# Pair 0's k on two queues, its two heads gated apart, and SyncE's loads beside the weights tied to VectorE

## Chip, core and metric

The kernel runs on one core of a Trainium2 chip. The metric is device time in microseconds for one launch. The kernel before has a median of 290.4 us over 3 runs (288.86 to 292.19). The engines are called as in the profile: PE (TensorE matmuls), PEld (its weight loads), DVE (VectorE), ACT (ScalarE), POOL (GpSimd) and SP (SyncE). SP, ACT and POOL can each issue DMAs on a queue of their own.

## What is computed

Block-sparse attention over q, k, v of 4 x 8 x 768 x 64, and on its output a Fourier mixing layer with an MLP.

```python
# attention: 12 blocks of 64 keys
k_rep = k.reshape(B, H, 12, 64, D).mean(axis=3)
gate = einsum('bhsd,bhnd->bhsn', q, k_rep)            # causal by block
mask = top 3 blocks of each row by gate, and its own block, and causal
attn = softmax(where(mask, q @ k.T / 8, -1e9)) @ v
x = attn.transpose(0, 2, 1, 3).reshape(4, 768, 512)
# per batch element
u = x + real(fft(fft(x, axis=1), axis=2))
un = (u - mean(u)) / sqrt(var(u) + 1e-6)
out = u + maximum(un @ w_ch1, 0) @ w_ch2
```

## The kernel before

Work goes in 16 pairs of heads, four pairs to a batch element. A pair takes these steps (function `attention`):

- Loads of k, q and v of both heads (`load`, issued from L655), on SP but for the first ones of q.
- Casts to f16 (L1017 is the helper for VectorE and POOL, L1016 for ACT) and low halves, so that q and k are kept as a high and a low f16 part (`tensor_tensor` at L768 for q, L773 for k).
- The turn of k and q on PE (L785, L851) through PSUM, or for pairs from 7 on with DMA transposes on SP (L793, L842).
- Block sums of k, `k_sums`: pairs 0 to 2 take the f32 keys straight into PE (L809, `sums32 = p < 3`), later ones the two f16 parts (L814). `spread` (L831) copies the sums.
- The gate: `gates` (L871, 20 small matmuls for both heads in one PSUM bank), two additions on VectorE (L894, L898), ten MAX8 (`tops`, L905), a comparison with the third largest (L923), the turn of the resulting mask on PE (`m_turn`, L933), and `spell`, which writes it into extra rows of turned q (L943). The heads share one buffer for each step.
- Six groups of `scores` per head (L967), the causal mask, the exponential on ACT (L979), and `attend` (L997) with its normalization (L1006, L1009). The causal mask is a PE matmul with a triangle for pairs 0 to 4 (L962, `on_pe = p < 5`) and an affine select on POOL after the exponential for later ones (L985).

After every fourth pair follow `fourier` (stage 1 at L1072, stage 2 at L1106 to L1118), the normalization (L1162, L1165, L1189, L1193), a turn of the normalized rows `unT` (PE, L1213, or a DMA transpose at L1205) and the MLP (`up`, L1316, `down`, L1345). The last two batch elements use a seven-product scheme for `down` (L1289). The weights arrive as 16 transfers of 256 KB on POOL's queue (`weight`, L659).

The order of all this is not written by hand. Every step is an `Op` with a rank, costs per engine, what it reads and writes, and for transfers a duration; `Plan.schedule` places them one by one on engines and PSUM banks with a model of time, steered by tables of tuned ranks and choices (`RANKS`, `RELS`, `TAKES`). The result is a fixed order per engine, and instructions then wait for their operands only. So the planner's start times order the work, but nothing holds an instruction back until its planned time, except waits on data. Two details matter here:

- Where the planner sees PE idle in the first 75 us, it notes a count of fillers (`o.fill`), and as many matmuls of 512 columns on a zero tile run there (`filler`, L677). A first block of 12 stands ahead of all work.
- The planner models the transfers of SP and POOL as sharing the DMA engines: an SP transfer beside a POOL transfer lasts up to six times as long (`SHARE`).

The functions that the change touches, with the lines of the profile:

Of the kernel before, what the change touches and what calls it, by code (L numbers as in the profile page):

```python
# [16 lines left out]
NEG = -60000.0  # L17
AF = mybir.ActivationFunctionType
OP = mybir.AluOpType

S = 768
DM = 512
NB = 12
NST = 6
# [62 lines left out]
class Plan:  # L87
# [8 lines left out]
    LANDING = 0.8  # L96
    TURN = dict(alone=0.4, early=1.5, mixed=0.5)
# [60 lines left out]
    def schedule(self):  # L158
        ops = self.ops
        free = dict(PE=1.0, ACT=1.5, DVE=0.9, POOL=1.3, SP=0.75)  # L160
# [21 lines left out]
        port_free, holder = 0.0, None  # L182
# [8 lines left out]
        while left:  # L191
# [63 lines left out]
            if o.dma or o.turn:  # L255
# [7 lines left out]
                if o.turn and shared == 0.0:  # L263
                    o.done = max(free[e] + 1.4, dma_free[mine] + 3.0)
                o.base = dma_free[mine] = go + took
                landing[e].append(o)
                flying[other] = [d for d in flying[other] if d.base > go]
# [36 lines left out]
SPELL = 7  # L304
WBR, HAR = 17000, 19000
STEP = 13.4

# [16 lines left out]
for _c in CHUNKS:  # L324
# [214 lines left out]
def kernel(  # L539
# [9 lines left out]
    nc = tc.nc  # L549
# [133 lines left out]
    for i in range(2):  # L683
        small(0.5, "DVE", 0.2, lambda x, n, i=i: nc.vector.memset(gmp[i], 0.0), w=[("gmp", i)])
# [740 lines left out]
```

## Time and profile before

| | us |
|---|---|
| median of 3 runs | 290.4 (288.86 to 292.19) |
| profiled execution | 288.77 |
| its span, first to last instruction | 287.1 |
| PE busy | 281.5 (98%) |
| DVE busy | 231.7 (81%) |
| ACT busy | 177.5 (62%) |
| POOL busy | 165.6 (58%) |
| DMA read and written | 28.58 MB and 6.29 MB |

A row of groups reads: line, engine, operation, what is written and read, shape, count, then busy time, mean duration in ns, and the idle time before with what ended it. A row of waits reads: who waited for whom, then us in total, how often, the longest. A row of the chain reads: start, duration, work. A row of stages reads: window, its length, busy time and count for PE, PEld, DVE, ACT and POOL, the granted PE clock, the DMA share and GB/s. A row of issues reads: what is loaded, queue, count, size, median us from issue to landing. PE's busy time counts fillers as work.

### The profile page before, as it was taken

How to read it: one execution, taken by the hardware profiler on the slowest of the kernel's cores; microseconds unless marked ns; L12 is line 12 of the kernel's file. 1: busy time of each engine (PE TensorE's matmuls, PEld its weight loads, DVE VectorE, ACT ScalarE, POOL GpSimd, SP SyncE). 2: the span in 40 equal slices, each digit the busy share in tenths (PEclk: the TensorE clock that was granted, in tenths of full speed). 3: DMA queues.
4: the chain of work that ended last, by engine and by line, in shares of the span. 5: the costliest groups of instructions: out<-in, count | busy, mean ns of one | idle time of the engine just before them, and what ended most of it. 6: DMA issues, size and time to landing. Idle time of an engine off the chain costs nothing.

```text
span 287.1 us, 8223 instructions
## 1 busy us (share of the span) xinstructions
PE 281.5 (98%) x3034; PEld 199.6 (70%) x3034; DVE 231.7 (81%) x783; ACT 177.5 (62%) x403; POOL 165.6 (58%) x300
## 2 busy tenths in 40 slices
PE   8999999999999999999999999999999999999995
PEld 4788877885656676566656686566677787866884
DVE  5678899889436788988564989999998999847895
ACT  2759988994734663987925596888775534365000
POOL 6587867926974734788889453754127972031300
PEclk9999999999999999999999999999999999999999
DMA  8999999999799889987899984563100032330032
GB/s 208 264 230 237 237 255 187 196 200 164 125 207 194 199 163 211 208 133 169 142 179 257 189 190 77 86 144 87 21 1 2 1 82 85 59 109 0 21 128 75
DMA packets 124057, 41.05 MB, mean 143 GB/s; under 512 B 115705, under 2 KB 120985, under 8 KB 124017
## 3 DMA queue, kind: packets, MB, share of 16 engines
q1 hardware_dynamic: 119536, 35.67, 59.6%
q0 software_dynamic: 3552, 4.56, 9.2%
q8 instruction: 24, 0.39, 0.6%
q10 hardware_dynamic: 928, 0.30, 0.4%
q14 instruction: 17, 0.13, 0.2%
HBM read 28.58 MB, written 6.29 MB: 121 GB/s over the span
## 4 chain that ended last, share of the span: by engine, by line
PE 88%; DVE 5%; ACT 5%; issue 1%; DVEq 0%; ACTq 0%
PE bank L1316 28%; PE bank L1345 14%; PE bank L1289 13%; PE bank L967 11%; PE bank L997 6%; PE bank L677 3%; ACT turned L979 2%; PE bank L1072 2%; PE bank L809 1%; PE bank L851 1%; PE bank L933 1%; PE bank L814 1%; PE bank L962 1%; PE bank L871 1%; ACT u L1016 1%
## 5 line engine op out<-in xcount | busy, mean ns | idle before, releaser
L979 ACT ACTIVATE turned<-bank 128x512 f16<-128x512 f32 (+1 forms) x192 | 89.2, 574 | 13.4 <-PE bank L967 13.3
L1316 PE MATMUL bank<-unT,w 128*128 128x384 f16 x512 | 89.2, 326 | 0.6 <-DVE unT L1017 0.5
L1328 ACT ACTIVATE hT<-bank 128x384 f16<-128x384 f32 x98 | 47.0, 492 | 38.6 <-PE bank L1316 38.0
L1316 PEld LDWEIGHTS <-w 128*128 128x128 f16 x512 | 48.6, 98 | 31.3 <-issue 1.5
L967 PE MATMUL bank<-turned,keys 76*128 76x128 f16 (+7 forms) x384 | 50.5, 259 | 0.0
L1345 PE MATMUL bank<-w,hT 128*128 128x512 f16 x192 | 46.9, 378 | 0.0
L967 PEld LDWEIGHTS <-keys 76*128 76x128 f16 (+1 forms) x384 | 28.8, 97 | 11.7 <-issue 0.4
L985 POOL TENSOR_SCALAR_AFFINE_SELECT turned<-turned 128x256 f16<-128x256 f16 (+1 forms) x44 | 22.4, 520 | 11.2 <-ACT turned L979 7.4
L1297 DVE TENSOR_TENSOR u<-u,bank 128x256 f32<-128x256 f32 x72 | 25.9, 413 | 3.6 <-PE bank L1289 2.3
L1345 PEld LDWEIGHTS <-hT 128*128 128x128 f16 x192 | 17.2, 97 | 15.8
L997 PEld LDWEIGHTS <-turned 128*128 128x128 f16 x672 | 23.8, 97 | 3.3
L1240 POOL TENSOR_TENSOR turned<-hT 128x384 f16<-128x384 f16 x14 | 12.5, 911 | 22.9 <-ACT hT L1328 12.3
L1289 PEld LDWEIGHTS <-turned 128*128 128x128 f16 x240 | 23.5, 98 | 2.9
L997 PE MATMUL bank<-small,turned 128*128 128x65 f16 x672 | 25.2, 193 | 0.0
L773 POOL TENSOR_TENSOR loads<-loads 128x384 f16<-128x384 f32 x24 | 21.9, 914 | 2.1 <-PE bank L814 1.2
L1017 POOL CAST small<-loads 128x384 f16<-128x384 f32 x28 | 13.9, 504 | 14.9 <-DMA loads<-in_v_dram 7.7
L1330 DVE TENSOR_SCALAR hT<-bank 128x384 f16<-128x384 f32 x30 | 16.5, 553 | 6.2 <-PE bank L1316 5.0
L943 DVE TENSOR_SCALAR turned<-bank 12x384 f16<-12x384 f16 (+2 forms) x50 | 18.2, 364 | 3.1 <-PE bank L933 1.8
L768 POOL TENSOR_TENSOR turned<-loads,turned 128x320 f16<-128x320 f32 x25 | 19.6, 792 | 1.5 <-DVE pm L1042 1.0
L1240 POOL TENSOR_TENSOR turned<-hT,hT 128x384 f16<-128x384 f16 x12 | 10.9, 913 | 15.6 <-DVE turned L1240 6.0
L1009 DVE TENSOR_TENSOR x<-bank,small 128x384 f16<-128x384 f32 x32 | 17.7, 553 | 0.5
L1289 PE MATMUL bank<-loads,turned 128*128 128x256 f16 x144 | 17.2, 273 | 0.0
(144 smaller groups left out, 491.1 us busy)
## 6 DMA issues: line engine op xcount, KB each, us to landing
loads<-in_k_dram SPq DMA_DIRECT2D x28, 192.0 KB, 3.8
loads<-in_v_dram SPq DMA_DIRECT2D x28, 192.0 KB, 3.6
loads<-in_q_dram SPq DMA_DIRECT2D x26, 192.0 KB, 3.8
w<-in_moe_w_ch_dram POOLq DMA_DIRECT2D x16, 256.0 KB, 8.4
out_dram<-u SPq DMA_DIRECT2D x12, 256.0 KB, 3.0
out_dram<-u SPq DMA_DIRECT2D x24, 128.0 KB, 1.7
hT<-in_k_dram SPq DMA_DIRECT2D x4, 192.0 KB, 3.8
hT<-in_q_dram SPq DMA_DIRECT2D x4, 192.0 KB, 3.9
```

The source lines that it names most:

```text
L768: lambda x, n, hi=hi, lo=lo, e=e: eng[x].tensor_tensor(out=lo, in0=qn[a][:, e, 1:NST], in1=hi[:, 1:NST], op=OP.subtract),
L773: lambda x, n, kh=kh, kl=kl, e=e: eng[x].tensor_tensor(out=kl, in0=kn[a][:, :, e, :], in1=kh, op=OP.subtract),
L967: nc.tensor.matmul(bank32[sp.bank][:, co:co + a1 - a0], KI[e][g3][0:ROWS[e], jt, :], QG[e][g3][0:ROWS[e], a0:a1], start=not added, stop=no ...
L979: lambda x, n, sp=sp, pt=pt, at=at, wid=wid: nc.scalar.activation(out=pt[:, at:at + wid], in_=bank32[sp.bank][:, 0:wid], func=AF.Exp, scal ...
L985: lambda x, n, pt=pt, at=at, nd=nd: nc.gpsimd.affine_select(out=pt[:, at:at + 128 * nd].rearrange("p (a c) -> p a c", a=nd), in_=pt[:, at: ...
L997: nc.tensor.matmul(o[:, st, 0:65], pt[:, col:col + 128], V16[v4][:, e, jt, 0:65], start=(i == 0), stop=(i == 20))
L1240: lambda x, n_: eng[x].tensor_tensor(out=dst, in0=x0, in1=x1, op=op),
L1289: nc.tensor.matmul(bank32[mp.bank][:, 0:256], lhs[:, z, :], rhs[:, z, :], start=(z == 0), stop=(z == 7))
L1297: lambda x, n, mp=mp, sign=sign, part=part: nc.vector.tensor_tensor(out=part, in0=part, in1=bank32[mp.bank][:, 0:256], op=sign),
L1316: nc.tensor.matmul(bank32[hp_.bank][:, 0:384], w1[:, dt, 128 * it:128 * it + 128], unT[:, dt, 384 * hf:384 * hf + 384], start=(dt == 0), s ...
L1328: nc.scalar.activation(out=o, in_=i_, func=AF.Relu)
L1345: nc.tensor.matmul(bank32[cp.bank], hT[hf][:, it, 128 * j:128 * j + 128], w2[:, it, :], start=(it == 0), stop=(it == NIT - 1))
```

## The change

It has these parts; the planner's tables of ranks and choices are replaced with it, so that the order on every engine is another.

1. First loads: k of both heads leads, one on SP's queue and one on ACT's; q of head 0 moves from ACT's queue to SP's second place. The first block of fillers has 8 matmuls for 12. POOL's constants may be issued earlier.
2. The planner's model of the first transfers (issued before 8 us) changes (`EARLY`): they land one after another over all queues.
3. `SPLIT = 1`: for pair 0 the gate runs per head, with a PSUM bank, additions, MAX8, comparison and turn for each, and with the second head's mask in the other mask buffer.
4. `sums32 = p < 2` and `on_pe = p < 4`: pair 2's block sums come from f16 parts, and pair 4's causal mask moves to POOL. The cast of pair 0's q may also run on ACT.
5. `HELD`: an SP instruction whose planned start lies between 36 and 76 us gets a wait on the VectorE instruction that the plan ends last before that start.

```diff
+    EARLY = 8.0
+    HELD = (36.0, 76.0)
...
-                o.fill = (0 if st < 6.5 else int(gap / 0.215) if st > 16.0 else
+                o.fill = (0 if st < 5.0 else int(gap / 0.215) if st > 16.0 else
...
-                if o.turn and shared == 0.0:
+                if st < self.EARLY:
+                    o.done = early = max(early, free[e] + (2.4 if e == "POOL" else 2.1)) + work
+                    shared, took = 0.0, o.done - self.AFTER[mine] - go
+                elif o.turn and shared == 0.0:
...
+SPLIT = 1
...
-    P.op(0, {"PE": 4.9}, lambda x, n: filler(12), r=["warm"], w=["spare"])
+    P.op(0, {"PE": 3.4}, lambda x, n: filler(8), r=["warm"], w=["spare"])
...
     load(0, 1, "k", 0)
-    load(0, -2, "q", 0, "ACT")
-    load(0, 1.2, "k", 1)
+    load(0, -2, "k", 1, "ACT")
+    load(0, 1.2, "q", 0)
...
-        on_pe = p < 5
-        sums32 = p < 3
+        on_pe = p < 4
+        sums32 = p < 2
...
+        for es in ((0,), (1,)) if p < SPLIT else ((0, 1),):
+            e0, e1 = es[0], es[-1] + 1
+            gi = (g2 + e0) % 2
+            gp = P.psum("tr")
+
+            def gates(x, n, es=es, gp=gp):
+                for e in es:
...
+            def tops(x, n, es=es):
+                for st in range(5):
+                    for e in es:
+                        nc.vector.max(out=mx8[g2][:, st, e, :], in_=gsb[g2][:, st, 12 * e:12 * e + 12])
...
+            if o.eng == "SP" and P.HELD[0] < o.start < P.HELD[1]:
+                by = max((d for d in P.ops if d.i in made and d.eng == "DVE" and
+                          made[d.i] is not None and d.done < o.start), key=lambda d: d.done)
+                tc.add_manual_dep(made[o.i].ins, made[by.i].ins.name, mybir.DependencyInfo(
+                    mybir.DependencyClass.Sync, mybir.DependencyReason.DATA), reason="held")
```

Over the whole program this takes 12 f32 passes of L809, four matmuls of L962 and five fillers out of PE's order (46 to 41) and adds 12 f16 matmuls of L814 and five transposes of L933; POOL gets four affine selects more (44 to 48).

More of the change, by code (lines that the diff above doesn't have):

```diff
@@ L159, in schedule @@
         ops = self.ops
-        free = dict(PE=1.0, ACT=1.5, DVE=0.9, POOL=1.3, SP=0.75)
+        free = dict(PE=1.0, ACT=0.8, DVE=0.9, POOL=1.3, SP=0.75)
         ready = {e: [] for e in free}
@@ L181, in schedule @@
         flying = dict(POOL=[], SP=[])
-        port_free, holder = 0.0, None
+        port_free, holder, early = 0.0, None, 0.0
         order = []
@@ L683 @@
     for i in range(2):
-        small(0.5, "DVE", 0.2, lambda x, n, i=i: nc.vector.memset(gmp[i], 0.0), w=[("gmp", i)])
+        small(0.5, "DVE", 0.2, lambda x, n, i=i: nc.vector.memset(gmp[i], 0.0),
+              w=[("gmp", i, 0), ("gmp", i, 1)])
     for i in range(NV):
@@ L733 @@
             dr["IndR"].ap().rearrange("n (s c) -> n s c", c=128),
-            [("kind", e, i) for i in range(NG)], 0.2, r=["kz"] if e == 0 else [], rel=4.0)
-    const(0.8, "POOL", ltri, dr["SM"].ap()[:, 392:520], ["sm2"], 0.3, 4.7)
+            [("kind", e, i) for i in range(NG)], 0.1, r=["kz"] if e == 0 else [], rel=2.3)
+    const(0.8, "POOL", ltri, dr["SM"].ap()[:, 392:520], ["sm2"], 0.1, 3.0)
     load(0, 1.87, "v", 0)
@@ L763, in attention @@
                   r=[("kn", a, e)], w=[("k16", h2, e)], port=True, rel=release(p))
-            small(base + 1, {"DVE": 0.37, "POOL": 0.52} if fast else {"POOL": 0.52}, 0,
+            small(base + 1, {"DVE": 0.37, "POOL": 0.52, "ACT": 0.46} if p == 0 else {"DVE": 0.37, "POOL": 0.52} if fast else {"POOL": 0.52}, 0,
                   lambda x, n, hi=hi, e=e: _copy(x, hi, qn[a][:, e]),
@@ L857, in attention @@
                   r=[tq], w=[("qg", e, g3), ("qm", e, g3)], ps=[tq])
-        gp = P.psum("tr")
-        def gates(x, n):
-            for e in range(2):
-                for st in range(1, NST):
-                    q_ = QG[e][g3][:, 128 * st:128 * st + 128]
-                    if wide:
-                        at = 48 * (st - 1) + 24 * e
-                        nc.tensor.matmul(bank32[gp.bank][:, at:at + 24], q_, G[g2][:, e, :],
-                                         start=True, stop=True)
-                        continue
-                    at = 24 * (st - 1) + 12 * e
-                    for i in range(2):
-                        nc.tensor.matmul(bank32[gp.bank][:, at:at + 12], q_,
-                                         G[g2][:, e, 12 * i:12 * i + 12],
-                                         start=(i == 0), stop=(i == 1))
@@ L874, in attention @@
-        P.op(base + 20, {"PE": 0.27 if wide else 0.54}, gates,
-             r=[("gh", g2)] + [(t, e, g3) for t in ("qg", "qm") for e in range(2)],
-             w=[gp], ps=[gp], pre=[("gsb", g2)])
-        half = lambda t: t.rearrange("p a (e n) -> p a e n", e=2)
-        raw = lambda: half(bank32[gp.bank][:, 0:120].rearrange("p (a c) -> p a c", a=5))
-        part = lambda i: bank32[gp.bank][:, 0:240].rearrange(
-            "p (a e i n) -> p a e i n", a=5, e=2, i=2)[:, :, :, i, :]
-        third = lambda: mx8[g2][:, :, :, 2:3].to_broadcast([128, 5, 2, NB])
@@ L926, in attention @@
-        gt = P.psum("tr")
-        by = 2 if p >= SPELL else 1
-        nj = 6 // by if by == 2 else 5
-        def m_turn(x, n):
-            for j in range(nj):
-                nc.tensor.transpose(bank16[gt.bank][0:64 * by, 128 * j:128 * j + 128],
-                                    gmp[g2][:, by * j:by * j + by, :].rearrange("p a c -> p (a c)"),
-                                    id16)
-        P.op(base + 24, {"PE": 0.06 * nj}, m_turn, r=["sm", ("gmp", g2)], w=[gt], ps=[gt])
-        for e in range(2):
-            def spell(x, n, e=e):
-                rows = QG[e][g3][64 - AT[e]:64 - AT[e] + NB, 128:S].rearrange("p (a c) -> p a c", a=5)
-                turned = bank16[gt.bank][:, 0:128 * nj].rearrange("p (j c) -> p j c", j=nj)
-                for i in range(by):
-                    at = 64 * i + 32 * e
-                    nc.vector.tensor_scalar(out=rows[:, i::by, :],
-                                            in0=turned[at:at + NB, 0:nj - i, :],
-                                            scalar1=-NEG, scalar2=NEG, op0=OP.mult, op1=OP.add)
-            small(base + 25, "DVE", 0.69 if by == 2 else 0.47, spell,
-                  r=[gt, ("qg", e, g3)], w=[("qm", e, g3)], ps=[gt])
```

136 lines of the change are left out of this document (90 added, 46 removed), and 381 rows, old and new, of tables (ACT, DVE, POOL, RANKS).

## The prediction

> **What bounds the kernel now.** I read the page first (busy shares, chain), then the waits of PE, then the table of stages, then the chain in the first 18 us and the transfers of 40 to 70 us.
>
> ```profile
> PE 281.5 (98%) x3034; PEld 199.6 (70%) x3034; DVE 231.7 (81%) x783; ACT 177.5 (62%) x403; POOL 165.6 (58%) x300
> ...
> PE 88%; DVE 5%; ACT 5%; issue 1%; DVEq 0%; ACTq 0%
> ```
>
> PE (TensorE) is busy for 281.5 of 287.1 us, and the chain that ended last lies on it for 88%. What PE waited for, as a list of all its waits:
>
> ```profile
> PE bank L677 <- DVE bsb L666: 1.3, 1, 1.3
> PE bank L1316 <- DVE unT L1017: 0.5, 1, 0.5
> PE bank L1213 <- DVE keys L1017: 0.4, 1, 0.4
> PE bank L1072 <- ACT small L1016: 0.2, 1, 0.2
> ```
>
> These four are 2.4 us, and 1.3 of them is the start. So PE's time is a sum of instructions: what leaves PE's order shortens the run, and a wait in PE's order lengthens it one for one. Part of this "work" is padding, though. The fillers (L677) are matmuls on zeros that the planner puts where it expects PE to be idle:
>
> ```profile
> L677 PE MATMUL bank<-bsb 128*128 128x512 f16 x46 | 13.7, 426 | 1.3 <-DVE bsb L666 1.3
> ```
>
> By stage (busy us of PE, PEld, DVE, ACT, POOL):
>
> ```profile
> 0.00:17.00 17.00, 15.73 (x152) 10.68 (x153) 11.16 (x66) 6.89 (x10) 10.63 (x26) 1.00 1.03 230
> 17.00:40.00 23.00, 22.96 (x407) 18.48 (x405) 19.59 (x74) 21.45 (x50) 17.84 (x30) 1.00 1.05 241
> 40.00:60.00 20.00, 19.82 (x266) 15.81 (x265) 18.45 (x64) 18.23 (x43) 16.90 (x27) 1.00 1.11 204
> 60.00:76.00 16.00, 15.18 (x170) 9.99 (x168) 12.39 (x45) 10.03 (x23) 9.04 (x17) 1.00 0.88 146
> ```
>
> From 17 to 40 us ACT's exponentials fill 21.45 of 23 us, so PE has little lead there. PE idles 0.18 us in 40 to 60 and 0.82 in 60 to 76.
>
> **The change, part by part.** The changed program has 41 fillers for 46: 8 ahead of the first real work for 12, and 33 later ones for 34. Of the later ones 15 stand ahead of pair 0's first scores for 17 before, and 18 behind them for 17.
>
> *The start.* Pair 0's key sums (L809) need both heads' k. Before, both k sit behind each other on SP's queue and q of head 0 heads ACT's; now k of head 1 heads ACT's queue.
>
> ```profile
> 1.27 4.57 PE bank L677 x12
> 5.84 1.30 PE bank L809 x12
> ...
> 12.75 1.94 PE bank L677 x9
> 14.69 0.40 PE bank L933 x5
> 15.09 0.60 PE bank L871 x20
> 15.69 1.34 PE bank L809 x12
> ```
> ```profile
> 0.82 0.48 ACTq L655 DMA_DIRECT2D loads<-in_q_dram  x1
> 0.82 1.03 SPq L655 DMA_DIRECT2D loads<-in_k_dram  x2
> ```
> ```profile
> loads<-in_q_dram ACTq DMA_DIRECT2D x1, 192.0 KB, 3.7
> loads<-in_k_dram SPq DMA_DIRECT2D x1, 192.0 KB, 3.3
> ```
> ```profile
> loads<-in_k_dram SPq DMA_DIRECT2D x1, 192.0 KB, 4.2
> ```
>
> The first rows give the issues, the others the time to landing: the heads of the two queues land at 0.8 + 3.3 = 4.1 and 0.8 + 3.7 = 4.5 us. The second k on SP, issued half-way through its 1.03 us, at 1.3, lands at 1.3 + 4.2 = 5.5. So both k are there at 4.5 instead of 5.5. Fillers start 0.42 us apart at first (rows below), so eight of them end at 1.27 + 8 x 0.42 = 4.65, when k is in. Twelve ended near 5.7, where the sums' first row stands.
>
> ```profile
> 4.24 0.15 PEld L677 LDWEIGHTS <-bsb 128*128 128x128 f16 x1 [0.28 <-issue]
> 4.66 0.15 PEld L677 LDWEIGHTS <-bsb 128*128 128x128 f16 x1 [0.28 <-issue]
> 5.03 0.32 PEld L677 LDWEIGHTS <-bsb 128*128 128x128 f16 x2 [0.22 <-issue]
> ```
>
> The start is 5.68 - 4.65 = 1.0 us earlier. But PE runs at half rate until about 5.03 us (0.42 us a filler against 1.94/9 = 0.216 later), and what now runs between 4.65 and 5.03 pays that: the sums lose half of 0.38, 0.2 us. Net 0.8 us gained. Counted as four fillers at 0.42 it would have been 1.7.
> The Trainium skill (TensorE: Matmul & The Clock Gate, "What's actually happening") says why: the warm-up is a budget of some 3.4 us of activity and not a number of matmuls, with a window that does not start with the kernel. This trace agrees, with 5.03 - 1.27 = 3.8 us, although the granted clock in the table of stages reads 1.00.
>
> *Heads gated apart (pair 0).* The gate matmuls stay 20 (10 and 10); the two heads' MAX8 stay 10; three VectorE instructions become six halves; the turn of the mask is done per head, so 5 more transposes of PE: at most 0.40 us, L933's row above. The VectorE halves run where PE had 9 fillers (the row at 12.75 us) and has 7 now, so these cover them; without that cover each would delay the mask's turn by its own length. One filler less in all: 0.2 us gained.
>
> *Pair 2's key sums in f16* (from `sums32 = p < 2`): 12 passes in f32 go, 1.34 us by the last L809 row, and 12 matmuls of two columns come, 0.28 us by the row below. 1.06 us gained. In exchange k's low halves are made by one more POOL and one more VectorE instruction.
>
> *Pair 4's causal mask* (from `on_pe = p < 4`): four PE matmuls go, two of 512 and two of 256 columns. L1345 streams 512 columns in 2.60/12 = 0.216 us (rows below), 256 take half: 0.65 us gained. POOL gets four affine selects.
>
> ```profile
> 79.69 0.28 PE bank L814 x12
> ...
> 83.30 2.60 PE bank L1345 x12
> ```
> ```profile
> L985 POOL TENSOR_SCALAR_AFFINE_SELECT turned<-turned 128x256 f16<-128x256 f16 (+1 forms) x44 | 22.4, 520 | 11.2 <-ACT turned L979 7.4 <-DVE small L824 0.9 <-DVE x L1193 0.9
> L773 POOL TENSOR_TENSOR loads<-loads 128x384 f16<-128x384 f32 x24 | 21.9, 914 | 2.1 <-PE bank L814 1.2 <-DVE fs L1029 0.9
> ```
>
> POOL's addition is 4 x 0.52 = 2.1 us for pair 4 and 0.9 for pair 2, at 17 to 60 us, where it has 23 + 20 - 17.84 - 16.90 = 8.3 us free. Bounds: 0 if it lies in those, 2.1 if all four selects delay pair 4's attend matmuls. With POOL as full as that PE idled only 0.18 us from 40 to 60; I take 0.2, nearest to that row.
>
> *The held transfers.* Seventeen issues of SP between the planner's 36 and 76 us get a wait on VectorE: the six loads of pair 7 and the six of pair 8, pair 7's four DMA transposes, and one transpose of the normalized rows. The first waits for pair 6's gate mask (L924 of the changed kernel). Everything later on SP queues behind it; pair 7's casts on POOL, and pair 7's key sums in PE's order, wait for it. SP before:
>
> ```profile
> 39.44 0.38 SPq L655 DMA_DIRECT2D loads<-in_k_dram  x1
> ...
> 45.21 10.81 SPq L655 DMA_DIRECT2D loads<-in_q_dram  x2
> 56.13 8.90 SPq L655 DMA_DIRECT2D loads<-in_k_dram  x2
> ```
> ```profile
> w<-in_moe_w_ch_dram POOLq DMA_DIRECT2D x14, 256.0 KB, 8.7
> loads<-in_q_dram SPq DMA_DIRECT2D x4, 192.0 KB, 14.5
> loads<-in_k_dram SPq DMA_DIRECT2D x3, 192.0 KB, 6.8
> ```
>
> Pair 7's loads went out at 39 to 45 us, among fourteen weight loads, and SP's landings took 6.8 to 14.5 us (medians of k and q). The planner had placed them at 61 us, which nothing enforced; now its places of 57 to 76 us for the seventeen are enforced by the waits. So pair 7's loads go out some 15 us later than they did, behind most of the weights' issues. PE idles 0.82 us in 60 to 76; the hold can give that back at most, and nothing at least if those waits (on VectorE's copies, second and third row of PE's waits) have nothing to do with transfers. I take half, 0.4. Its loss is a rival below.
>
> **The sum.** -0.8 (start) - 0.2 (one filler) - 1.06 - 0.65 + 0.40 (turns) + 0.2 (POOL) - 0.4 (hold) = -2.5 us. The profiled execution has 288.77 us, span 287.1; it becomes 286.3. The runs shown have a median of 290.4 (288.86 to 292.19), 1.6 over the profiled one; the forecast for the median is 290.4 - 2.5 = 287.9.
>
> **Rivals.**
> *The held loads land late (slower).*
>
> ```profile
> 65.89 7.31 PE bank L1316 x44
> ```
>
> Pair 7's key sums now stand behind 13 groups of `up` (four L1316 matmuls, 4 x 7.31/44 = 0.66 us), six score groups (up to 512 columns, 0.22 us) and two attends (21 matmuls of 65 columns each, at L1345's rate 0.58 us) counted from the first `up`: 8.6 + 1.2 + 1.2 = 11.0 us. The first `up` was at 65.9 and is some 2 us earlier now, so the sums are due at 75. POOL's low halves (0.91 us each, L773's row) and the casts ahead of them take some 2.8 us, an estimate; the loads must be in by 72. Issued at 58 to 62 they land at 65 to 69 with k's 6.8 us, which leaves 3 us, and at 73 to 77 with q's 14.5, which makes PE 1 to 5 us late: it takes its order as it stands. It decides once the loads are over 5.4 us late (2.5 gained, and 2.9 for 1%). With 14.5 us and a last issue at 65, if VectorE is late too, they are 7.5 late: 287.9 + 7.5 = 295.4. For it: SP's slow rows. Against: at 58 few weights fly.
> *The clock stays low.* If k or q come late, PE is idle just as its rate is to rise, and a second low stretch follows: 3.8 us at half rate, 1.9 us lost, 289.8. For it: the padding ahead of the key sums is cut to eight. Against: the head of ACT's queue landed at 4.5.
> By the same section of the Trainium skill (TensorE: Matmul & The Clock Gate) an idle window puts the clock back; a second stretch of its 3.4 us would cost 1.7 us, an estimate, and no run here shows one.
> *The early start is given back.* From 17 to 40 us ACT has 1.55 us free. If it sets the pace to 40 us, what is gained ahead of that (0.8 + 0.2 + 1.06) only makes PE wait: -0.4 remains, 290.0. For it: the changed order has 8 fillers where pair 2 is, which had 4. Against: those are in the count already, and ACT too starts earlier.
> *The hold also takes the runs' spread.* If PE's 1.0 us of idle time from 40 to 76 goes whole, POOL costs nothing, and the median comes down to the profiled execution: 288.77 - 2.3 - 1.0 = 285.5. For it: three runs differ by 3.3 us, and SP's landings among weights by as much. Against: no row ties the two together.
>
> **How the numbers follow.** Forecast 0.50, with its own range 286.2 to 289.2; loads late 0.10; clock low 0.10; given back 0.12; spread taken 0.18. About 1% (2.9 us) is what a measurement of this kernel can tell from no change: 287.5 and 293.3 are the bounds. Faster: 0.28 of the forecast and 0.18, together 0.46. Slower: 0.10. Within 1%: 0.44. The range leaves out the late loads and a tail below: 285.3 to 290.9.
>
> **What would show it.** Right: the first key sums at 4.6 to 4.8 us and the first scores near 14 us instead of 15.69 + 1.34 = 17.0, since pair 2's key sums and pair 1's gates no longer stand ahead of them; twelve L809 passes fewer; SP's first issue for pair 7 near 58 us, with landings under 8 us; PE idle under 1 us in 40 to 76. Wrong: a wait of PE on DMA or POOL near 75 us (late loads), fillers or sums 0.4 us apart after 5.5 us (clock), PE waiting for ACT between 17 and 40 us (given back).

## The result, and the profile after

The changed kernel has a median of 292.25 us (289.6 to 297.33, 20 executions) and the kernel before, measured beside it, 290.41 us (288.86 to 293.35, 20 executions). The ratio of the two is 1.005, with an interval of 1.0027 to 1.0074. It is slower by half a per cent, less than the 1% that separates two kernels here, and 2.5 us of forecast gain are missing. Executions over 1.5% above the fastest of their kernel are left out of the ratios (4 of 20 of the changed kernel, 1 of 20 of the kernel before), and where a profile below is of such an execution (e2, e11 and f3) only its start is read. The profiled execution after took 290.25 us, span 288.5, against 288.77 and 287.1 before.

Busy time and the chain that ended last, from the page after:

```profile
PE 280.8 (97%) x3030; PEld 198.5 (69%) x3030; DVE 229.8 (80%) x784; ACT 176.9 (61%) x402; POOL 173.2 (60%) x309
...
PE 75%; DVE 8%; DMA 7%; ACT 5%; POOL 2%; issue 2%; SPq 0%; DVEq 0%; ACTq 0%; POOLq 0%
```

PE lost only 0.7 us of busy time, and its share of the chain fell from 88% to 75%: DMA, DVE and POOL now stand on the path. What PE waited for, after:

```profile
PE bank L881 <- DMA turned<-turned: 1.5, 3, 1.2
PE bank L685 <- DVE bsb L674: 1.3, 1, 1.3
PE bank L1121 <- ACT tr L1031: 0.5, 1, 0.5
PE bank L1331 <- DVE x L1024: 0.4, 1, 0.4
PE bank L860 <- ACT turned L994: 0.3, 1, 0.3
PE bank L1228 <- ACT turned L994: 0.2, 1, 0.2
PE bank L1331 <- DVE u L1153: 0.2, 1, 0.2
```

The four waits of before (2.4 us) have become seven (4.4 us). The largest is new: L881, the gate of pairs that are turned by DMA transposes. The stages after (columns as before):

```profile
17.00:40.00 23.00, 22.59 (x410) 18.02 (x409) 19.93 (x80) 21.14 (x49) 19.63 (x31) 1.00 1.00 232
40.00:60.00 20.00, 19.38 (x300) 15.57 (x297) 18.39 (x75) 18.04 (x42) 15.65 (x30) 1.00 1.06 185
60.00:76.00 16.00, 15.79 (x180) 10.95 (x177) 11.72 (x33) 14.54 (x33) 12.84 (x20) 1.00 0.96 190
76.00:140.00 64.00, 62.47 (x621) 39.52 (x620) 44.36 (x159) 39.49 (x94) 40.52 (x83) 1.00 0.94 184
```
```profile
76.00:140.00 64.00, 63.98 (x676) 41.66 (x675) 47.54 (x160) 42.53 (x104) 43.88 (x88) 1.00 0.95 184
```

The last row is of the kernel before. Length less busy time is PE's idle time: 0.04 became 0.41 us in 17 to 40, 0.18 became 0.62 in 40 to 60, 0.82 became 0.21 in 60 to 76, and 0.02 became 1.53 in 76 to 140.

A busy PE can still be slow, so idle time is not all. To see both, each PE instruction is counted at the usual distance to its successor in the kernel before (the median of its kind), and the rest of the time is called lost. That count is an arithmetic on the whole trace, and an estimate. It gives some 274.5 us of work before and 272 after: the work fell by 2.5 us. The lost time rose by 4.0 us: 0.5 from 5 to 18 us, 1.2 from 18 to 70, 1.95 from 70 to 140, 0.3 after that.

The start, in the chain of the first 18 us, after:

```profile
1.27 3.60 PE bank L685 x8
4.87 1.57 PE bank L818 x12
...
11.51 1.51 PE bank L685 x7
...
14.61 0.22 PE bank L982 x2
```

Eight fillers, the sums right behind them, first scores near 14.5 us as forecast. SP's queue after:

```profile
59.28 0.38 SPq L663 DMA_DIRECT2D loads<-in_v_dram  x1
...
67.95 0.51 SPq L663 DMA_DIRECT2D loads<-in_v_dram  x1
68.76 2.25 SPq L851 DMA_TRANSPOSE turned<-turned  x1
```
```profile
SPq L663 <- DVE small L1180: 21.0, 1, 21.0
```
```profile
loads<-in_q_dram SPq DMA_DIRECT2D x4, 192.0 KB, 5.1
loads<-in_k_dram SPq DMA_DIRECT2D x3, 192.0 KB, 5.4
```

The hold did what it says: SP stood for 21.0 us behind one wait on VectorE, pair 7's loads went out from 59 us, and they landed in 5.1 to 5.4 us (medians from 40 to 72 us) and not in 6.8 to 14.5.

### The profile page after: what moved, and what is told of

The parts are those of the page before. It is cut to its first block, busy times and chain, and to the rows that moved or that the text cites. A ratio compares the mean times of both kernels' runs of the same rounds, so it can differ in the third digit from the quotient of the medians.

```text
span 288.5 us, 8239 instructions
## 1 busy us (share of the span) xinstructions
PE 280.8 (97%) x3030; PEld 198.5 (69%) x3030; DVE 229.8 (80%) x784; ACT 176.9 (61%) x402; POOL 173.2 (60%) x309
## 4 chain that ended last, share of the span: by engine, by line
PE 75%; DVE 8%; DMA 7%; ACT 5%; POOL 2%; issue 2%; SPq 0%; DVEq 0%; ACTq 0%; POOLq 0%
PE bank L1331 21%; PE bank L1360 13%; PE bank L1304 13%; PE bank L982 10%; PE bank L1012 6%; DMA turned<-turned 3%; PE bank L685 3%; ACT turned L994 2%; DMA hT<-in_k_dram 2%; DMA loads<-in_v_dram 2%; PE bank L860 1%; PE bank L948 1%; DVE x L1024 1%; PE bank L818 1%; PE bank L823 1%
## 5 line engine op out<-in xcount | busy, mean ns | idle before, releaser
L994 ACT ACTIVATE turned<-bank 128x512 f16<-128x512 f32 (+1 forms) x192 | 90.4, 579 | 20.8 <-PE bank L982 20.2
L1331 PE MATMUL bank<-unT,w 128*128 128x384 f16 x512 | 90.9, 326 | 0.6 <-DVE x L1024 0.4
L1343 ACT ACTIVATE hT<-bank 128x384 f16<-128x384 f32 x95 | 46.4, 501 | 39.6 <-PE bank L1331 34.6
L1331 PEld LDWEIGHTS <-w 128*128 128x128 f16 x512 | 48.0, 97 | 30.2 <-issue 1.3
L982 PE MATMUL bank<-turned,keys 128*128 128x128 f16 (+7 forms) x384 | 51.3, 258 | 0.2
L1000 POOL TENSOR_SCALAR_AFFINE_SELECT turned<-turned 128x512 f16<-128x512 f16 (+1 forms) x48 | 24.7, 524 | 17.1 <-ACT turned L994 7.7
L1255 POOL TENSOR_TENSOR turned<-hT 128x384 f16<-128x384 f16 x14 | 12.6, 912 | 22.7 <-ACT hT L1343 18.4
L1345 DVE TENSOR_SCALAR hT<-bank 128x384 f16<-128x384 f32 x33 | 18.3, 554 | 9.5 <-PE bank L1331 8.1
L1032 POOL CAST turned<-loads 128x384 f16<-128x384 f32 x25 | 12.6, 508 | 12.4 <-DVE fs L1069 8.7
L1032 POOL CAST small<-loads 128x384 f16<-128x384 f32 x24 | 12.1, 508 | 13.0 <-DMA loads<-in_v_dram 4.3
L1255 POOL TENSOR_TENSOR turned<-hT,hT 128x384 f16<-128x384 f16 x13 | 11.8, 914 | 11.8 <-DVE turned L1255 5.5
```

The lines of the kernel that those rows point to most:

```text
L982: nc.tensor.matmul(bank32[sp.bank][:, co:co + a1 - a0], KI[e][g3][0:ROWS[e], jt, :], QG[e][g3][0:ROWS[e], a0:a1], start=not added, stop=no ...
L994: lambda x, n, sp=sp, pt=pt, at=at, wid=wid: nc.scalar.activation(out=pt[:, at:at + wid], in_=bank32[sp.bank][:, 0:wid], func=AF.Exp, scal ...
L1000: lambda x, n, pt=pt, at=at, nd=nd: nc.gpsimd.affine_select(out=pt[:, at:at + 128 * nd].rearrange("p (a c) -> p a c", a=nd), in_=pt[:, at: ...
L1032: return eng[x].tensor_copy(out=dst, in_=src)
L1255: lambda x, n_: eng[x].tensor_tensor(out=dst, in0=x0, in1=x1, op=op),
L1331: nc.tensor.matmul(bank32[hp_.bank][:, 0:384], w1[:, dt, 128 * it:128 * it + 128], unT[:, dt, 384 * hf:384 * hf + 384], start=(dt == 0), s ...
```

## The experiments

Three theories stood against each other. *Hold*: the wait on SP costs more than it brings. *Start*: with eight fillers and k on both queues, PE's rate rises late in many executions. *Order*: the new order, and the work given to POOL, return what PE saves as waits on other engines. Ratios are to the kernel before, with a 95% interval.

### How well one comparison repeats

e0 is the changed kernel, unchanged, a second time.

> The changed kernel once more, beside the three that follow. All theories: 1.003 to 1.008 of the kernel before; PE waits for DMA transposes at the gate matmuls (L881), 1 to 2 us in all, and for ACT and VectorE between 30 and 66 us, some 2 us in all.

Measured: 291.27 us, ratio 1.0032 (1.0004 to 1.0061); PE's waits at L881 are 0.9 us in its profile. Three kernels were measured twice, on different chips. The changed one gave 1.0050 and 1.0032. The one without the hold (e1, e11) gave 0.9977 and 1.0005. The one of e5 and f6 gave 0.9974 and 1.0053, with intervals that do not meet. So a kernel's ratio moves by 0.2 to 0.8% from one measurement to the next, which the interval of one measurement does not cover. Below, a cause is called shown only where several kernels agree or where the profile has the place.

### The hold

e1 and e11: the changed kernel with

```diff
-    HELD = (36.0, 76.0)
+    HELD = (0.0, 0.0)
```

> The changed kernel without the waits of SP on VectorE (HELD = 0 to 0); the order on every engine is the same. Theory 'order' (the new order leaves the DMA transposes and ACT's exponentials too little time ahead of PE): PE's waits stay within 0.7 us of the changed kernel's, and the time within 0.3%. Theory 'hold' (held loads hand their lateness on to pair 7's transposes and all that follow): the waits at L881 near 81, 97 and 115 us go, and the time falls by 1.5 to 2 us, under the kernel before. If the hold does what it is written for, pair 7's loads go out from about 40 us instead of 59, land after 10 us and more, and the time rises by up to 1 us.

Measured: 0.9977 (0.9951 to 1.0003), 0.55% (1.6 us) under e0, measured beside it.

> The changed kernel without the hold once more: 0.995 to 1.000 of the kernel before. Theory 'hold': PE waits for DMA transposes at the gates of pairs 7 to 9 for under 1 us in all between 70 and 140 us. Theory 'order': over 1.5 us in this execution too.

Measured: 1.0005 (0.9978 to 1.0031). e6 does the reverse and gives the kernel before the same wait:

```diff
+    HELD = (36.0, 76.0)
...
+            if o.eng == "SP" and P.HELD[0] < o.start < P.HELD[1]:
+                by = max((d for d in P.ops if d.i in made and d.eng == "DVE" and
+                          made[d.i] is not None and d.done < o.start), key=lambda d: d.done)
+                tc.add_manual_dep(made[o.i].ins, made[by.i].ins.name, ...)
```

> The kernel before with the hold alone (same rule, same range of the planner's time); the order on every engine is the same. Theory 'hold' (held loads hand their lateness on to the DMA transposes behind them): slower by 0.3 to 0.7%, PE waits for DMA transposes or POOL between 70 and 140 us, over 1.5 us idle there for 0.8 before. Theory 'fit' (only the changed order has no time left for it): within 0.3%.

Measured: 1.0043 (1.0014 to 1.0071). The stages of 60 to 140 us of e6, then of e1:

```profile
60.00:76.00 16.00, 15.18 (x174) 10.30 (x172) 12.93 (x46) 10.44 (x23) 8.18 (x16) 1.00 0.96 184
76.00:140.00 64.00, 62.36 (x656) 40.14 (x655) 46.53 (x158) 40.28 (x97) 42.58 (x86) 1.00 0.96 184
```
```profile
60.00:76.00 16.00, 15.79 (x195) 11.13 (x193) 11.85 (x33) 14.84 (x35) 12.26 (x23) 1.00 0.73 128
76.00:140.00 64.00, 63.81 (x648) 40.58 (x644) 46.30 (x163) 41.05 (x98) 42.62 (x85) 1.00 0.90 184
```

In the order of before, the hold leaves the 0.82 us of 60 to 76 as they were and puts 1.64 us of idle time into 76 to 140. In the new order without it, 60 to 76 has 0.21 us all the same, and 76 to 140 has 0.19 instead of 1.53. So the new order took the idle time of 60 to 76, the hold none of it. f3 holds the loads alone, f4 (with `o.turn` for `not o.turn`) the DMA transposes alone:

```diff
-            if o.eng == "SP" and P.HELD[0] < o.start < P.HELD[1]:
+            if o.eng == "SP" and not o.turn and P.HELD[0] < o.start < P.HELD[1]:
```

> The changed kernel with the wait on VectorE left on the twelve loads of pairs 7 and 8 and taken from the DMA transposes. If the loads held back (and what queues behind them) are what costs: ratio as the changed kernel, 1.003 to 1.005, TensorE idle in 70 to 140 us near 2.5 us. If the wait of the transposes themselves costs: as without the hold, 0.998 to 1.0005, idle there near 0.7 to 1.5 us.

> The changed kernel with the wait left on the DMA transposes alone (pair 7's four and one of the normalized rows) and taken from the loads. If the held loads cost: 0.998 to 1.0005 and idle time in 70 to 140 us near 0.7 to 1.5 us. If the held transposes cost: 1.003 to 1.005 and idle time near 2.5 us.

Measured: f3 1.0035 (1.0005 to 1.0065), f4 1.0016 (0.9991 to 1.0042). The idle time of 76 to 140 alone does not prove the price, since e1 and f4 reach that stage more than 1 us later than the changed kernel (their start, next section). Two waits of PE that all kernels of the new order share make a measure without the start: the first at L1121, for ACT's copy in the first Fourier layer, and the one at L1331, for VectorE, near 179 us. From the second to the last matmul all eight need 106.0 us (in e8 the lines are L1126 and L1336).

| | loads held | wait at L1121 ends, us | wait at L1331 ends, us | between |
|---|---|---|---|---|
| after | yes | 56.44 | 179.19 | 122.75 |
| e0 | yes | 56.05 | 178.50 | 122.45 |
| f4 | no (transposes held) | 57.65 | 179.50 | 121.85 |
| e1 | no | 57.48 | 178.75 | 121.27 |
| e5 | no | 56.63 | 177.95 | 121.32 |
| e8 | no | 56.51 | 177.94 | 121.43 |
| f6 | no | 59.11 | 180.67 | 121.56 |
| e4 | no | 57.25 | 180.65 | 123.40 |

The stretch is some 1.1 us longer where the loads are held (mean 122.6) than in five of the six kernels where they are not (mean 121.5). The sixth, e4, has no hold and is the longest, with these waits for transposes:

```profile
PE bank L881 <- DMA turned<-turned: 1.8, 3, 0.8
```

So PE can wait there without a hold too. Over all: the changed kernel with the loads held (after, e0, f3) has a mean ratio of 1.0039, the same order without (e1, e11, e4, e5, f4, f6, of which e4, e5 and f6 have more fillers) 1.0005. By this the hold costs 0.34% or 1.0 us there, and 0.43% or 1.2 us in e6.

How a hold that ends at 76 us makes PE wait at 96 to 118 us shows in e6. One transpose in SP's queue, of before and of e6, and the waits of PE that e6 has and the kernel before has not:

```profile
92.23 1.29 SPq L842 DMA_TRANSPOSE turned<-turned  x1
```
```profile
95.17 1.29 SPq L843 DMA_TRANSPOSE turned<-turned  x1
```
```profile
PE bank L867 <- DMA turned<-turned: 0.8, 1, 0.8
...
PE bank L1317 <- DMA unT<-x: 0.5, 1, 0.5
...
PE bank L968 <- DMA keys<-loads: 0.4, 1, 0.4
```

The same transpose goes out 2.9 us later, and PE's wait of 0.8 us ends when it has landed. Of these 2.9 us, 1.0 are not the hold's: in this execution PE's rate rose late, and every matmul from 17 to 90 us stands 1.0 us later than before. The three new waits on transposes make 1.7 us. In the changed kernel the queue does not explain the price: from 79 to 110 us SP issues every transpose within 0.2 us of e1's time. The longest wait, 1.2 us at 115 us, is for a transpose that SP issued at the same time after and in e1:

```profile
109.86 1.45 SPq L851 DMA_TRANSPOSE turned<-turned  x1
```
```profile
109.83 1.21 SPq L851 DMA_TRANSPOSE turned<-turned  x1
```

By the trace it landed 5.4 us later after and 3.3 us later in e1, but 5.4 us later in e4 as well. Why it took longer stays open.

### The start

e4 takes e1 and puts the old first block back (`filler(12)` for `filler(8)`). e5 and f6 take e1 and add two fillers to each of the paddings that are planned between 5 and 9 us:

```diff
-            filler(o.fill)
+            filler(o.fill + 2 if o.fill and 5.0 < o.start < 9.0 else o.fill)
```

> The changed kernel without the hold, and with 12 fillers in the first block as before the change. Theory 'clock' (from 5 to 11 us PE now streams too little, and in a part of the executions its rate falls back to half from 11 us on): with the padding back the rate holds, PE's idle and slow time between 5 and 18 us is under 0.8 us in the profile (2.7 in the profile without the hold), the slowest of a dozen executions is under 292 us, and the fastest is 0.5 to 1.0 us slower than the 287.6 without it, since the key sums start one us later. Theory 'chance' (the slow start has nothing to do with the padding): executions of 294 us and more come as often as before.

> The changed kernel without the hold, with two more fillers at each of three places between 5 and 9 us (six, 1.3 us at most, of which some 0.5 us lie in PE's idle time). Theory 'clock': as with 12 fillers, no execution over 292 us, and a median of 288 to 289 us. Theory 'chance': the spread stays, and the median rises by 0.8 us over the 288.9 without the six.

> The changed kernel without the hold and with two fillers more in each block of padding planned between 5 and 9 us, measured a second time. If this is a version that beats the kernel before: ratio 0.995 to 0.999 with an interval below 1. If the new order gives back what leaves TensorE's order whatever the hold and the padding: 0.999 to 1.001.

Measured: e4 1.0004 (0.9982 to 1.0026), e5 0.9974 (0.9937 to 1.001), f6 1.0053 (1.0029 to 1.0077). Theory 'clock' had no execution over 292 us in e4 and e5; they reach 297.91 and 294.38. If their long executions are ones with a late rate, as the profiles of e2, e11 and f3 below are, more padding alone does not prevent it. e8 takes e1, puts the old load places back (q of head 0 on ACT's queue, both k on SP's) and twelve fillers:

```diff
+        if p == 0 and (what, e) in (('k', 1), ('q', 0)):
+            named = ("kn" if what == "k" else "qn", i, e)
+            what, e = ('q', 0) if (what, e) == ('k', 1) else ('k', 1)
```

> The changed kernel without the hold and with the old start: q of head 0 at the head of ACT's queue, k of head 1 second on SP, 12 fillers; the order is otherwise the same. The prediction's working gives 0.8 us more than without the hold alone. Theory 'clock' (what is run between 5 and 18 us decides, and there the changed order has fewer matmuls that stream): the median is within 0.5 us of the kernel without the hold, because fewer executions lose time at the start. Theory 'gain' (the early key sums bring their 0.8 us): 0.5 to 1.0 us slower than without the hold.

Measured: 0.9995 (0.998 to 1.0011), and no execution over 290.2 us. The chains of the first 18 us of e8 and of f6:

```profile
1.27 4.34 PE bank L685 x12
...
15.02 0.22 PE bank L987 x2
```
```profile
4.87 2.35 PE bank L818 x12
...
7.88 1.71 PE bank L685 x4
...
18.03 0.22 PE bank L982 x2
```

In f6 nothing waits for k. But its fillers from 7.88 us are still 0.43 us apart, and its first scores come 3.4 us after those of the changed kernel. The full rate came at 10.5 us instead of 5. e1 shows the same later on; its chain, then the stage:

```profile
11.88 2.93 PE bank L685 x7
```
```profile
11.00:14.00 3.00, 3.00 (x18) 1.56 (x15) 1.50 (x16) 2.80 (x5) 1.86 (x3) 0.53 1.18 265
```

Seven fillers take 2.93 us and not 1.51, and here the granted clock shows it, with 0.53. In e2, e11 and f3 it lasts longest; the same fillers in e11's chain:

```profile
15.96 2.99 PE bank L685 x7
```

So of ten profiles of the new order with eight fillers at the head, four have the full rate from about 5 us on (after, e0, e3, e5), three are at half rate at 10 or 12 us (e1, f4, f6), and three still at 18 us. In the eight profiles with twelve (the kernel before, e4, e6, e8, e10, f1, f2, f5) the rate is full by 8 us, though the sums behind them start anywhere from 5.65 (e8) to 6.57 us (e6, f2). First scores, by the trace, with eight fillers and k on both queues: 14.45 (after), 14.56 (e0), 14.73 (e3), 16.23 (e1), 16.41 (f4), a mean of 15.3. In e2, e11 and f3 they come at 20.6 to 20.7. With twelve and the old loads (e8): 14.85. The new start gains 0.1 to 0.4 us over e8 when the rate rises early and loses 1.4 to 1.6 us, or nearly 6, when it does not. That it gains nothing on average is what these profiles suggest; e8 is one execution, and its fillers ended earliest of the eight with twelve.

Three kernels try the start in the order of before. e7 exchanges k of head 1 with q of head 0 in SP's and ACT's queues and has eight fillers; there q stood ahead of the other k on SP, so that one k landed at 5.4 us, not earlier. e9 puts each k at the head of a queue, with eight fillers, and e10 is the same with twelve (without the last two lines):

```diff
+        if p == 0 and (what, e) in (('k', 0), ('q', 0)):
+            named = ("kn" if what == "k" else "qn", i, e)
+            what, e = ('q', 0) if (what, e) == ('k', 0) else ('k', 0)
...
-    P.op(0, {"PE": 4.9}, lambda x, n: filler(12), r=["warm"], w=["spare"])
+    P.op(0, {"PE": 4.9}, lambda x, n: filler(8), r=["warm"], w=["spare"])
```

> The kernel before with the new start alone: k of both heads ahead on two queues, q of head 0 second on SP, 8 fillers for 12; the order is otherwise the same. The prediction's working gives 0.8 us less. Theory 'clock': the fastest execution gains 0.3 to 0.8 us, but a part of them falls to half rate at 8 to 12 us, so the spread grows to over 5 us and the median is not lower. Theory 'chance': every execution gains the 0.8 us.

> The kernel before with the new start, and this time with k of both heads at the heads of the two queues (in the run before this one q of head 0 stood ahead of k on SP); 8 fillers, order otherwise the same. Theory 'gain': the key sums start at 4.7 us, and the time falls by 0.5 to 0.8 us (0.997 to 0.998). Theory 'clock': PE's rate rises late or falls back in some executions: PE idle and slow for over 1.5 us between 5 and 18 us in the profile or a granted clock under 1, and a ratio of 1.000 to 1.006.

> The same with 12 fillers as before the change: only the two loads change places. Theory 'gain': k is in long before the padding ends at 5.7 us, so nothing is gained or lost: within 0.2%. Theory 'clock': the same, since the padding is whole; if it is slower by 0.3% and more, it is the order of the loads (q later) that costs, not the padding.

Measured: e7 1.0069 (1.0033 to 1.0104), e9 1.004 (1.0012 to 1.0068), e10 1.0013 (0.9996 to 1.0031). e7's chain shows PE's rate where k comes late and padding is short:

```profile
5.52 2.69 PE bank L814 x12
8.21 1.73 PE bank L677 x4
```

The sums take 2.69 us for 1.3 and the fillers stand 0.43 us apart. e9 and e10 differ in four fillers alone and by 0.27%, with intervals that overlap, so that the short block costs in the order of before too is likely but not shown: in e9's one profile the rate rose early, and its scores come 0.4 us ahead of e10's. e10, whose padding is whole, had nothing to gain from the early k. e9 and e10 share a wait at 166 us that the kernel before does not have (here of e10):

```profile
PE bank L819 <- POOL loads L778: 1.7, 1, 1.7
```

Why two loads exchanged at 1 us make POOL late there was not found. Nor is it known how often it comes: e10's profile is of its longest execution, 291.22 us, and its median is 289.61.

### The causal mask on POOL, and the new order

e2 is the changed kernel with pair 4's mask back on PE (POOL's four selects left out), e3 the changed kernel with the gates of the pairs from 7 on, and what hangs on them, placed 1.3 us later in the plan:

```diff
-                    added = nd and on_pe
+                    added = nd and p < 5
...
-                          lambda x, n, pt=pt, at=at, nd=nd: nc.gpsimd.affine_select(
+                          lambda x, n, pt=pt, at=at, nd=nd: None if p == 4 else nc.gpsimd.affine_select(
```
```diff
+            P.ops[-1].late = p >= 7
...
-        for o in P.place(RANKS, RELS, TAKES):
+        for o in P.shifted(1.3):
```

> The changed kernel with pair 4's causal mask back on PE: four matmuls more (0.65 us), four affine selects on POOL fewer (2.1 us); the order is otherwise the same. Theory 'order': the waits of 30 to 66 us stay but for some tenths, and the time rises by 0.3 to 0.7 us. Theory 'mask' (the selects on POOL delay attends and the Fourier stage behind them): the waits of 45 to 66 us fall by over 0.7 us and the time falls by up to 1 us.

> The changed kernel with the gate matmuls of pairs 7 to 15 placed 1.3 us later in the order, and behind them only what depends on them. Theory 'order': PE's waits for DMA transposes at L881 fall from 1.5 us to under 0.4, and the time falls by 1 to 1.5 us, to 0.998 to 1.003 of the kernel before. Theory 'hold': the transposes are late for good reason and the wait comes back in another place (mask, scores of the same pair); the time stays within 0.5 us of the changed kernel.

Measured: e2 1.0055 (1.0028 to 1.0082), e3 1.0082 (1.0055 to 1.0108). e2 lies 0.23% (0.7 us) over e0, which fits the 0.65 us of the forecast, but the intervals overlap. e3 is no faster, and its profile shows the wait moved and not removed. Its new wait of PE:

```profile
PE bank L966 <- POOL gmp L951: 1.2, 3, 0.8
```

f1, f2 and f5 try the mask in the order of before, where nothing else moves. f1 takes pair 4's mask off PE and gives it to POOL, f2 those of pairs 3 and 4 (3 for 4 in both places), f5 gives pair 4's to POOL and leaves it on PE as well (without the first two lines):

```diff
-                    added = nd and on_pe
+                    added = nd and p < 4
...
-                      lambda x, n, sp=sp, pt=pt, at=at, wid=wid: nc.scalar.activation(
+                      lambda x, n, sp=sp, pt=pt, at=at, wid=wid, nd=nd: (nc.scalar.activation(
                           out=pt[:, at:at + wid], in_=bank32[sp.bank][:, 0:wid], func=AF.Exp,
-                          scale=0.125),
+                          scale=0.125), cut(pt, at, nd) if nd and 4 <= p < 5 else None)[0],
```

Here `cut` is the affine select of L985. In f1, f2 and f5 it stands in POOL's order where the exponential before it stands in the program; no plan chose its place.

> The kernel before with nothing but pair 4's causal mask moved from TensorE to GpSimd; the order of everything else, the padding and the loads stay. Theory 'the work taken out of TensorE's order is worth its price, and the new order, the hold and the short padding eat it': four matmuls of L962 less, -0.65 us, ratio 0.9978, the fillers at 46, TensorE's waits after 40 us as before. Rival 'any work taken out comes back as a wait, since another engine sets the pace': ratio 1.000, with TensorE waiting for GpSimd's selects or ScalarE's exponentials between 40 and 60 us.

> The same for pairs 3 and 4: eight matmuls less, eight selects more. By the first theory -1.3 us, ratio 0.9955; by the rival 1.000 or above, as GpSimd has 8.3 us free from 17 to 60 us and gets 4.2 us of selects there.

> The kernel before with pair 4's causal mask applied twice: TensorE keeps its four matmuls of L962, and GpSimd gets the same four selects as in the run before of this kind. If GpSimd's selects hold up what follows them: ratio 1.005 to 1.008, TensorE idle near 1 us in 40 to 60 us (0.18 before). If the freed TensorE time only turned into waiting there, with the selects costing nothing: 0.999 to 1.002, idle below 0.4 us.

Measured: f1 1.0053 (1.0032 to 1.0074), f2 1.0146 (1.0121 to 1.017), f5 1.0046 (1.0026 to 1.0065). Both f1 and f2 are slower by more than the mask's time on PE. f5 shows which half does it: the selects cost 0.46% (1.3 us) by themselves, and with the 0.65 us of matmuls taken away on top (f1) the ratio is no lower, though intervals of 0.2% either way could hide a part of it. The stage of 40 to 60 us, first of f5, then of f1, then of f2:

```profile
40.00:60.00 20.00, 19.38 (x267) 15.28 (x265) 18.33 (x63) 17.68 (x43) 18.33 (x30) 1.00 1.12 200
```
```profile
40.00:60.00 20.00, 19.06 (x267) 15.04 (x265) 18.32 (x63) 17.78 (x43) 18.43 (x30) 1.00 1.15 203
```
```profile
40.00:60.00 20.00, 18.05 (x249) 13.75 (x246) 18.36 (x59) 16.80 (x39) 19.20 (x32) 1.00 1.02 182
```

POOL goes from 16.90 us before to 18.3, 18.4 and 19.2 of 20, and PE idles 0.62, 0.94 and 1.95 us for 0.18. The place is stage 1 of the Fourier layer; PE's wait there, of before, of f5 and of f1:

```profile
52.34 0.24 PE L1072 MATMUL bank<-small,fs 128*128 128x193 f16 x1 [0.18 <-ACT small L1016]
```
```profile
53.22 0.24 PE L1079 MATMUL bank<-small,fs 128*128 128x193 f16 x1 [0.62 <-ACT small L1023]
```
```profile
53.25 0.24 PE L1079 MATMUL bank<-small,fs 128*128 128x193 f16 x1 [0.62 <-ACT small L1023]
```

With and without the mask's matmuls PE passes this place at nearly the same time, 0.9 us later than before, and waits 0.62 us for the same copy. A part of the 0.9 us is the start: in these executions the rate rose later, and the first scores come 0.30 (f5) and 0.45 us (f1) after those of before. That leaves 0.6 us to the selects in f5. In f1, which has lost the mask's matmuls too, 0.5 us are left, so they bring 0.1 us of their 0.65 here; 0.26 of the rest stands at 47.8 us, as a wait of PE for VectorE's comparison (L923).

The copy waits for a cast on VectorE, and the elementwise instruction (a sum or difference of two operands) that VectorE has to finish ahead of that cast is longer. That instruction, of before and of f5, and what POOL does beside it in f5:

```profile
50.61 0.55 DVE L1054 TENSOR_TENSOR fs<-pm 128x768 f16<-128x768 f16 x1
```
```profile
51.06 0.98 DVE L1061 TENSOR_TENSOR fs<-pm 128x768 f16<-128x768 f16 x1
```
```profile
50.93 0.70 POOL L951 TENSOR_SCALAR_AFFINE_SELECT turned<-turned 128x512 f16<-128x512 f16 x1 [0.21 <-ACT turned L986]
```

Before, POOL only issued DMAs at that time. It takes 0.43 us more beside the select, and PE's wait is 0.44 us longer. So what PE pays at this place is not POOL's share of the stage but a VectorE instruction that is longer beside a POOL instruction. In the planned order of the changed kernel the selects have other places, and e2 shows no such price.

## Why the prediction was wrong, point by point

It forecast 287.9 us and faster; the kernel is at 292.25 and slower. The step that failed is its first: "PE's time is a sum of instructions: what leaves PE's order shortens the run". Its terms for PE alone (-0.8 - 0.2 - 1.06 - 0.65 + 0.40) are 2.3 us less, and the count has 2.5 us less; that work left PE's order and shortened nothing. The changed order without the hold stands at 1.0005, and what PE no longer does came back as waits and as matmuls at half rate. PE at 98% busy was read as PE being the only limit. But POOL had 16.90 of 20 us in 40 to 60, ACT 21.45 of 23 in 17 to 40, and the order placed their work to be ready just when PE needed it; that this is true at all the places is inferred from the waits, not shown for each.

- *Start, -0.8.* The mechanism came as forecast (sums at 4.9 us by the chain, first scores at 14.5). But the forecast took the moment at which the rate rises, 5.03 us, from one execution, as if it were fixed. It varies: with eight fillers at the head it was late, or fell back, in six of ten profiles of the new order. The term is near 0, not -0.8, by the profiles of the executions in the ratios, and a loss by the other three.
- *One filler, -0.2, and the split of pair 0.* The counts are as forecast: 41 fillers, and 67 transposes in L948 for 62 in L933. Neither was tried alone. In the changed profile nothing waits at pair 0's gate.
- *Pair 2's sums in f16, -1.06.* The passes are gone (24 in f32 for 36). This part was not undone by itself; no run shows its price.
- *Pair 4's mask, -0.65, and POOL, +0.2.* In the order of before the selects cost 1.3 us by the ratio (0.6 us at the Fourier layer by the trace) and the matmuls saved next to nothing: the upper bound of 2.1 us was nearer than the 0.2 taken. The sum priced POOL's free time and the attends, and had no term for VectorE instructions made longer beside a select. In the new order, which was planned with them, the move may be worth its 0.65 us (e2 against e0), within what one measurement can tell.
- *Hold, -0.4.* Wrong in sign: it costs 1.0 to 1.2 us by the ratios. The 0.6 us gained in 60 to 76 us are the new order's. The loads landed fast, as said, but that time was not needed.
- *Rival "the held loads land late".* Its mechanism, a hold that PE pays for, was right and its place wrong. The loads of pair 7 were early enough, landing some 5 us after issues from 59 us on. PE waits for DMA transposes instead: in e6 for those that queue behind, at 96 to 118 us; in the changed kernel at 81 to 115 us, where the queue is not late and the cause stays open. It was priced by the lateness of the loads alone, and costs 1 us without any.
- *Rival "the clock stays low".* Right, and not by a late k or q alone: in f6 no wait stands ahead of the slow stretch. It was priced at 1.9 us, and e1, f4 and f6 lose some 2.5 us more than the kernel before in 5 to 18 us by the count above; the profile after, 0.5.
- *Rival "the early start is given back".* Partly right. The new waits for ACT's exponentials (L860, 0.3 us at 32 us) and ACT's copy in the Fourier layer (L1121, 0.5 us at 56 us) are of this kind, the first not in e0. Of the 0.9 us by which the first scores after come ahead of e5's (14.45 and 15.37 us), 0.2 are left at the wait at 56 us (56.44 and 56.63). e8, with no hold and the old start, isolates the order: 1.6 us less work by the count, and a ratio of 0.9995. So the order alone returns all that its PE work saves, at several small places; the waits in e8's profile are 0.24 us for ACT at 33 us, 0.49 for ACT at 57, 0.21 for ACT at 66, 0.40 for a DMA transpose at 81 and 0.38 for VectorE at 178.
- *Rival "the hold also takes the runs' spread".* It did not come: 289.6 to 297.3 us, against 288.9 to 293.4 before.

The missing part, 2.5 us forecast and 1.5 us lost, is thus about 1.0 to 1.2 us from the hold, and the rest from the start and from the order's own waits, which the runs do not separate, with a scatter of 0.2 to 0.8% between measurements. No version was shown to beat the kernel before: e1 and e5 looked faster by 0.25% once and did not when repeated.

## What to carry to other kernels

When one engine is 98% busy in a schedule that was planned for all of them, its removed instructions are not a gain until what the other engines deliver at the same places has been read. Work moved to another engine has a price beyond that engine's free time: here an elementwise VectorE instruction was 0.43 us longer beside a select on POOL, and PE waited for what hung on it. A wait that holds an in-order queue can be paid by what queues behind it, as in e6 at 96 to 118 us for loads held until 63 us. And a padding whose job depends on the moment of the run is measured over many executions, by their spread as well as their median, before its length is called spare.

## What the runs showed of the hardware

- The moment at which PE's full rate starts is not fixed by the padding: it was about 5 us (after) and 10.5 us (f6) with the same first 8 fillers and no wait for k between, in e11 fillers of half rate still run at 18 us, and in e1 fillers of half rate stand from 11.9 to 14.8 us after sums that ran at full rate. By the Trainium skill (TensorE: Matmul & The Clock Gate, "What's actually happening") some 3.4 us of sustained activity release the rate in a window that does not start with the kernel. Eight fillers last 3.6 us in f6 and did not suffice; what follows them there are two-column f32 sums and transposes.
- The granted clock in the table of stages does not always show it. In f6 the fillers are 0.43 us apart while the row reads 1.00:

```profile
8.00:11.00 3.00, 3.00 (x14) 1.54 (x13) 1.12 (x3) 0.71 (x1) 1.47 (x3) 1.00 1.12 253
```

- SP's transfers beside the weights take 5.1 to 5.4 us when issued from 59 us on and 6.8 to 14.5 us when issued from 39 us on, and that difference of up to 9 us was worth nothing to PE.
- An elementwise VectorE instruction on two operands over 128x768 f16 took 0.55 us while POOL issued DMAs and 0.98 us beside a POOL select of 0.70 us (before and f5).
